# Attention and two feed-forward layers on one core: where the value sum's cast stands, and which engine converts the first weights

## The chip, the cores and the metric

The kernel runs on one core of a Trainium2 chip. The metric is the device time of one execution in microseconds (us), as the median of several runs. TensorE (PE) does the matrix products into PSUM, ScalarE (ACT) and VectorE (DVE) do the elementwise work, SyncE (SP) issues nearly all transfers. GpSimd (POOL) is idle but for the first microsecond.

## What is computed

```python
scores = scale * np.matmul(q, k.transpose(0, 1, 3, 2)) - np.log(S)
attn = 1.0 / (1.0 + np.exp(-scores))
attn_out = np.matmul(attn, v)              # batch 4, 12 heads, S = 448, head size 64
x = attn_out.transpose(0, 2, 1, 3).reshape(B * S, H * D)      # 1792 x 768
h = x @ w_in;   x = (h - np.tanh(h)) @ w_out                  # 768 -> 2048 -> 768
h = x @ w_in2;  out = (s * np.maximum(h, 0) ** 2 + b) @ w_out2
```

The weights arrive as 64-bit floats; all else is 32-bit.

## The kernel before

The work is done in two halves `sb` of two batches each. A half runs attention for 12 steps `i` (a step is one batch and a pair of heads), then `layer1`, then `layer2`, all on 896 rows. Every operation is recorded in the order in which the code is written, engine by engine (class `InOrder`, line 80, so all instructions of a profile carry the line L80). Products that have to be accurate are split: an operand is a rounded part `hi` and a rest `lo = t - hi`, and three products are summed.

One step `i` of attention (lines 490 to 506) runs, in this order:

- `qk(i, 0)` and `qk(i, 1)`: six products each into a PSUM tile `sc` and one sigmoid each on ScalarE, which writes `af`.
- in a few steps of the first half, `w_load`, `w_conv` or `w_split` for the first weights (line 495).
- `prep(i + 1)`: seven transposes of the next q and k into a PSUM tile `tqk`, two casts on ScalarE (`qt`, `kt`), and on VectorE two subtractions and the copy `qkf`. The tile is free again after that copy.
- `av(i - 1)` up to its `yield`: the value sum `o` of the step before, and a part `o2` of it in another bank.
- `qk(i, 3)`: four small products and a sigmoid of half the size.
- the rest of `av(i - 1)`: ScalarE copies `o2` to `half`, VectorE adds it to `o`, ScalarE casts `o` into `x`, VectorE subtracts for the rest of `x`.
- `qkv_load(i + 3)`: nine small transfers on SyncE's queue for the step after next but one.
- `qk(i, 2)`.

The tiles `sc` and `tqk` share three PSUM buffers of two banks (tag `two`), taken in turn; `o` and `o2` share two single banks (tag `one`). So each use of a `two` buffer waits for the reader of the use three before it: `prep(i + 2)` for the sigmoid of `qk(i, 2)`, `qk(i + 1, 0)` for the copy `qkf` of `prep(i + 1)`.

A weight piece of 128 x 768 goes through `w_load` (raw 64-bit words, 768 KB), `w_conv` (the 64-bit float to 32 bits: `wy` is the high word scaled, `wa` and `wf` put the bits together, and `wf` is stored to memory for the second half) and `w_split` (`whi`, `wlo`). The first pieces are converted while the first half's attention runs:

```python
for at, step, n in ((2, w_load, 1), (4, w_load, 2), (5, w_conv, 0), (6, w_split, 0), (7, w_load, 3), (7, w_conv, 1), (8, w_split, 1), (9, w_load, 4), (9, w_conv, 2)):
    if i == at:
        now(upto(step, n))
```

Of the kernel before, what the change touches and what calls it, by code (L numbers as in the profile page):

```python
# [9 lines left out]
F32 = mybir.dt.float32  # L10
F32R = mybir.dt.float32r
U32 = mybir.dt.uint32
AF = mybir.ActivationFunctionType
ALU = mybir.AluOpType
# [5 lines left out]
def tile_kernel(ctx, tc, q, k, v, w_in1, w_out1, w_in2, w_out2, s_in, b_in, out):  # L20
# [61 lines left out]
    pe, act, dve, pool, sp = (InOrder(e) for e in (nc.tensor, nc.scalar, nc.vector, nc.gpsimd, nc.sync))  # L82

    def banks(name):
        return ps_p.tile([P, 2, 512], F32, tag="two", name=name, bufs=3)
# [11 lines left out]
    def w_src(key):  # L97
        kind, layer, a, b = key
        if kind == "in":
            return words[2 * layer][:, a * P:(a + 1) * P, :].rearrange("(c p) f t -> p c f t", p=P)  # L100
        return words[2 * layer + 1][a * 2 * P:(a + 1) * 2 * P, b * HM:(b + 1) * HM, :].rearrange("(c p) f t -> p c f t", p=P)
# [6 lines left out]
    chunks = a_pass * (B // 2)  # L108
    scratch, raw_t, f_t, w_t = {}, {}, {}, {}

    def w_load(n):
        if n >= len(chunks):
            return
        key = chunks[n]
        if key not in scratch:
            t = w_p.tile([P, WE, 2], U32, tag="raw", name="raw", bufs=3)
            a = CC if key[0] == "in" else 2
            sp.dma_start(out=t.rearrange("p (a f) t -> p a f t", a=a), in_=w_src(key))
            raw_t[n] = t
        else:  # L120
            t = w_p.tile([P, WE], F32, tag="wf", name="wf", bufs=5)
            sp.dma_start(out=t, in_=scratch[key])
            f_t[n] = t

    def w_conv(n):

        if n >= len(chunks) or n in f_t:
            return
        key = chunks[n]
        r = raw_t.pop(n)
        a = w_p.tile([P, WE], U32, tag="wa", name="wa", bufs=2)
        y = w_p.tile([P, WE], F32, tag="wy", name="wy", bufs=2)
        t = w_p.tile([P, WE], F32, tag="wf", name="wf", bufs=5)
        act.activation(y, r[:, :, 1].bitcast(F32), AF.Copy, scale=2.0 ** -112)  # L140
        yield
        dve.tensor_scalar(a, r[:, :, 0], 29, None, op0=ALU.logical_shift_right)
        yield
        dve.scalar_tensor_tensor(out=a, in0=y.bitcast(U32), scalar=3, in1=a, op0=ALU.logical_shift_left, op1=ALU.bitwise_or)
        dve.scalar_tensor_tensor(out=t.bitcast(U32), in0=y.bitcast(U32), scalar=0x80000000, in1=a, op0=ALU.bitwise_and, op1=ALU.bitwise_or)
        scratch[key] = dram.tile([P, WE], F32, name=f"w{key[0]}{key[1]}_{key[2]}_{key[3]}")
        sp.dma_start(out=scratch[key], in_=t)
        f_t[n] = t

    def w_split(n):  # L150
        if n >= len(chunks):
            return
        t = f_t.pop(n)
        hi = w_p.tile([P, WE], F32R, tag="whi", name="whi", bufs=4)
        lo = w_p.tile([P, WE], F32R, tag="wlo", name="wlo", bufs=4)
        act.copy(hi, t)
        yield
        dve.tensor_tensor(out=lo, in0=t, in1=hi.bitcast(F32), op=ALU.subtract)
        w_t[n] = (hi, lo)

    done = {w_load: 0, w_conv: 0, w_split: 0}

    def upto(step, n):

        while done[step] <= n:
            yield from step(done[step]) or ()
            done[step] += 1

    def w_ahead(n, parts="ab"):

        yield from upto(w_load, n + 5)
        for part in parts:
            if part == "a":
                yield from upto(w_conv, n + 3)
            else:
                yield from upto(w_split, n + 2)

    def now(g):
        for _ in g:
            pass  # L180
# [7 lines left out]
    def split(hi, lo, t):  # L188
        act.copy(hi, t)
        dve.tensor_tensor(out=lo, in0=t, in1=hi.bitcast(F32), op=ALU.subtract)  # L190
# [67 lines left out]
    def qk(i, c):  # L258

        b = i // NP  # L260
        qt, kt = ready[i]
        sc = banks("sc")
        if c == NJ:

            f = flt.pop(i)
            kl, qf = (f[:, 0:RM], f[:, RM:]) if b % 2 else (f[:, S:], f[:, 0:S])
            for h in range(2):
                for e in range(2):
                    hs = slice(e * D, e * D + D)
                    pe.matmul(sc[h * RM:h * RM + RM, e, :SH], kl[hs], qf[hs, h * SH:h * SH + SH], start=True, stop=True)  # L270
            avs[i].append(g_p.tile([P, 2, 2, S], F32, tag="g", name="af", bufs=4))
            act.activation(avs[i][-1][:, 1, :, :SH], sc[:, :, :SH], AF.Sigmoid, bias=nlogs, scale=SCALE)
            return
        k0 = c * P if b % 2 else c * P + RM
        for n, (wi, xi) in enumerate(((0, 0), (0, 1), (1, 0))):
            for e in range(2):
                hs = slice(e * D, e * D + D)
                pe.matmul(sc[:, e, :S], kt[hs, wi, k0:k0 + P], qt[hs, xi], start=n == 0, stop=n == 2)
        if c == 0:
            avs[i].append(g_p.tile([P, 2, 2, S], F32, tag="g", name="af", bufs=4))  # L280
        act.activation(avs[i][-1][:, c % 2], sc[:, :, :S], AF.Sigmoid, bias=nlogs, scale=SCALE)

    def av(i):

        b, hp = i // NP, i % NP
        rv, af = raws.pop(i)["v"], avs.pop(i)
        o = ps_p.tile([P, 512], F32, tag="one", name="o", bufs=2)[:, :S]

        o2 = ps_p.tile([P, 512], F32, tag="one", name="o2", bufs=2)[:, :SH]
        for c in range(NJ):  # L290
            for e in range(2):
                pe.matmul(o[e * D:e * D + D], rv[:, e, c, :], af[c // 2][:, c % 2, e], start=c == 0, stop=False)
        for h in range(2):
            for e in range(2):
                ks = slice(h * RM, h * RM + RM)
                pe.matmul((o2 if h else o[:, :SH])[e * D:e * D + D], rv[ks, e, NJ, :], af[1][ks, 1, e, :SH], start=h == 1, stop=True)
        yield
        half = tmp_p.tile([P, WN], F32, tag="t1", name="half", bufs=2)[:, :SH]
        act.copy(half, o2)
        dve.tensor_tensor(out=o[:, SH:], in0=o[:, SH:], in1=half, op=ALU.add)  # L300
        if b % 2 == 0:
            x_t[b // 2, hp] = x_p.tile([P, 2, T2], F32R, tag="x", name="x1", bufs=CC)
        ns = slice(b % 2 * S, b % 2 * S + S)
        xt = x_t[b // 2, hp]
        split(xt[:, 0, ns], xt[:, 1, ns], o)
# [182 lines left out]
    for sb in range(B // 2):  # L488
        i0, i1 = sb * 2 * NP, (sb + 1) * 2 * NP
        for i in range(i0, i1):  # L490
            if i == 0 or i > i0:
                qk(i, 0)
                qk(i, 1)

            for at, step, n in ((2, w_load, 1), (4, w_load, 2), (5, w_conv, 0), (6, w_split, 0), (7, w_load, 3), (7, w_conv, 1), (8, w_split, 1), (9, w_load, 4), (9, w_conv, 2)):
                if i == at:
                    now(upto(step, n))
            if i + 1 < i1:
                prep(i + 1)
            a = av(i - 1) if i > i0 else iter(())  # L500
            next(a, None)
            qk(i, 3)
            now(a)
            qkv_load(i + 3)
            qk(i, 2)
            ready.pop(i)
        order = [(0, range(CC - 2)), lambda: now(av(i1 - 1)), (1, range(CC - 1)), (0, range(CC - 2, CC)), (1, [CC - 1])]

        turn[0] = 3
        x2 = layer1(sb, order)  # L510
        last = sb + 1 == B // 2
        order = [(0, range(CC - 1)), (1, range(CC - 1)), (0, [CC - 1]), (1, [CC - 1])]
        layer2(sb, x2, order, {} if last else {2: lambda: prep(i1), 4: lambda: qk(i1, 0), 6: lambda: qk(i1, 1)})
# [30 lines left out]
```

## Time and profile before

| | |
|---|---|
| time, median of 3 runs | 1125.86 us (1124.82 to 1127.56) |
| profiled execution, time | 1124.64 us |
| its span on the core | 1122.8 us |
| granted TensorE clock, mean | 1.0 |
| TensorE busy | 1098.6 us (98%) |
| VectorE busy | 585.5 us (52%) |
| ScalarE busy | 493.7 us (44%) |

Busy times come from one execution, which the hardware profiler recorded; its span leaves 1.84 us of its time outside. A busy TensorE is not TensorE at its peak, since products are pipelined and their ends are modelled; idle time on it is the better guide. The first half's attention runs from the start to about 95 us, the second half's from about 570 to 649 us.

### The profile page before, as it was taken

What the parts mean: (1) busy time and instruction counts of PE and PEld (TensorE: products, weight loads), DVE (VectorE), ACT (ScalarE), POOL (GpSimd) and SP (SyncE); (2) the same over time, 40 slices, a digit from 0 to 9 for tenths busy, and PEclk for the clock granted to TensorE, in tenths of its full rate; (3) what the DMA queues carried; (4) which work ended last, traced back from release to release, by engine and by line L of the source; (5) the groups of instructions that cost most, each with busy time, mean ns of one, the idle gap of its engine ahead of it and who ended that gap; (6) DMA issues with size and microseconds to landing.
All of it is one profiled execution on the core that took longest, in us unless ns stands there. A gap on an engine that the chain in (4) does not pass through costs nothing.

```text
span 1122.8 us, 15139 instructions
## 1 busy us (share of the span) xinstructions
PE 1098.6 (98%) x6077; PEld 949.4 (85%) x6077; DVE 585.5 (52%) x878; ACT 493.7 (44%) x782; POOL 0.7 (0%) x6
## 2 busy tenths in 40 slices
PE   8899999999999999999998899999999999999998
PEld 4446889888889999898964578898888899999998
DVE  3453656767787668686633332343434541434343
ACT  5775444242446563635356643332313363515060
POOL 0000000000000000000000000000000000000000
PEclk9999999999999999999999999999999999999999
DMA  4765454546455645454444301121211121211102
GB/s 112 201 152 148 156 185 154 169 146 192 127 169 168 203 136 183 133 189 130 167 113 113 79 29 57 48 66 43 71 43 46 54 71 43 60 53 57 57 15 99
DMA packets 115430, 124.47 MB, mean 111 GB/s; under 512 B 56480, under 2 KB 90784, under 8 KB 115360
## 3 DMA queue, kind: packets, MB, share of 16 engines
q1 hardware_dynamic: 114416, 123.27, 36.6%
q8 instruction: 48, 0.79, 0.3%
q10 hardware_dynamic: 944, 0.23, 0.1%
q14 instruction: 22, 0.18, 0.0%
HBM read 92.80 MB, written 30.67 MB: 110 GB/s over the span
## 4 chain that ended last, share of the span: by engine, by line
PE 92%; DMA 3%; DVE 2%; ACT 2%; SPq 1%; issue 1%; ACTq 0%; DVEq 0%
PE h L80 42%; PE z L80 21%; PE y L80 20%; PE o L80 6%; PE sc L80 2%; PE tqk L80 2%; SPq L80 1%; ACT af L80 1%; DMA rawq<-in_q_dram 1%; DMA rawv<-in_v_dram 1%; DMA rawk<-in_k_dram 1%; DMA win<-wf 1%; DVE wa L80 0%; DVE o L80 0%; DVE qt L80 0%
## 5 line engine op out<-in xcount | busy, mean ns | idle before, releaser
L80 PE MATMUL h<-x,whi 128*128 128x512 f32 (+1 forms) x1536 | 434.4, 363 | 0.0
L80 PEld LDWEIGHTS h<-x,whi 128*128 128x128 f32 x1536 | 283.4, 188 | 33.9 <-issue 1.3
L80 PE MATMUL h<-x,wlo 128*128 128x512 f32 (+1 forms) x768 | 279.8, 364 | 0.0
L80 PE MATMUL z<-whi,g 128*128 128x384 f32 x896 | 229.5, 334 | 0.0
L80 PE MATMUL y<-g,whi 128*128 128x512 f32 (+1 forms) x768 | 218.6, 366 | 0.2 <-DVE y L80 0.2
L80 ACT ACTIVATE t<-h 128x512 f32<-128x512 f32 (+1 forms) x128 | 69.6, 544 | 234.3 <-PE h L80 233.7
L80 PEld LDWEIGHTS z<-whi,g 128*128 128x128 f32 x896 | 162.0, 188 | 0.6 <-issue 0.6
L80 PEld LDWEIGHTS y<-g,whi 128*128 128x128 f32 x768 | 142.4, 188 | 17.7 <-DVE y L80 0.6
L80 PEld LDWEIGHTS h<-x,wlo 128*128 128x128 f32 x768 | 144.1, 188 | 15.2
L80 DVE TENSOR_TENSOR wlo<-wf,whi 128x768 fp32r<-128x768 f32 x128 | 122.0, 953 | 59.7 <-ACT whi L80 59.7
L80 ACT CAST whi<-wf 128x768 fp32r<-128x768 f32 x128 | 106.1, 833 | 101.9 <-DVE wf L80 58.0
L80 PE MATMUL z<-wlo,g 128*128 128x384 f32 x448 | 149.7, 334 | 0.0
L80 PE MATMUL y<-g,wlo 128*128 128x512 f32 (+1 forms) x384 | 140.9, 367 | 0.0
L80 DVE TENSOR_TENSOR g<-t,g 128x512 fp32r<-128x512 f32 (+1 forms) x128 | 79.9, 624 | 83.5 <-ACT g L80 83.5
L80 ACT ACTIVATE af<-sc,nlogs 128x896 f32<-128x896 f32 (+1 forms) x96 | 83.1, 919 | 48.4 <-PE sc L80 39.0
L80 ACT CAST g<-t 128x512 fp32r<-128x512 f32 (+1 forms) x128 | 72.7, 568 | 33.2 <-DVE t L80 30.9
L80 DVE TENSOR_TENSOR t<-h,t 128x512 f32<-128x512 f32 x64 | 39.9, 623 | 85.4 <-ACT t L80 85.4
L80 PEld LDWEIGHTS z<-wlo,g 128*128 128x128 f32 x448 | 84.1, 188 | 0.0
L80 PEld LDWEIGHTS y<-g,wlo 128*128 128x128 f32 x384 | 72.1, 188 | 8.9 <-DVE wlo L80 0.4
L80 DVE TENSOR_TENSOR z<-z 128x384 f32<-128x384 f32 x84 | 45.2, 554 | 65.8 <-PE z L80 65.8
L80 PE MATMUL o<-af,rawv 128*64 128x448 f32 (+1 forms) x480 | 72.4, 478 | 0.0
L80 DVE TENSOR_TENSOR y<-y 128x512 f32<-128x512 f32 x72 | 41.5, 618 | 58.0 <-PE y L80 58.0
(42 smaller groups left out, 674.9 us busy)
## 6 DMA issues: line engine op xcount, KB each, us to landing
raw<-in_moe_w_in_dram SPq DMA_DIRECT2D x32, 768.0 KB, 5.2
raw<-in_moe_w_out_dram SPq DMA_DIRECT2D x32, 768.0 KB, 4.8
win<-wf SPq DMA_DIRECT2D x32, 384.0 KB, 2.6
wout<-wf SPq DMA_DIRECT2D x32, 384.0 KB, 2.6
wf<-win SPq DMA_DIRECT2D x32, 384.0 KB, 3.0
wf<-wout SPq DMA_DIRECT2D x32, 384.0 KB, 3.0
rawq<-in_q_dram SPq DMA_DIRECT2D x48, 96.0 KB, 2.7
rawv<-in_v_dram SPq DMA_DIRECT2D x24, 192.0 KB, 2.7
```

The costliest lines, as they stand in the source:

```text
L80: return lambda *a, **kw: tc.keep_in_program_order(getattr(self.engine, name)(*a, **kw))
```

## The change

Two edits. In `av` a second `yield` stands behind the addition of `half`; the loop over the steps runs `av(i - 1)` in three pieces now, and the last piece (cast and subtraction) follows `qk(i, 2)` instead of going ahead of it. And the weight steps that run inside the attention loop get `alone=True`, with which the scaling to `wy` and the cast to `whi` are done on VectorE instead of ScalarE. Calls of the same steps from the layers are as before.

```diff
-    def w_conv(n):
+    def w_conv(n, alone=False):
...
-        act.activation(y, r[:, :, 1].bitcast(F32), AF.Copy, scale=2.0 ** -112)
+        if alone:
+            dve.tensor_scalar(y, r[:, :, 1].bitcast(F32), 2.0 ** -112, None, op0=ALU.mult)
+        else:
+            act.activation(y, r[:, :, 1].bitcast(F32), AF.Copy, scale=2.0 ** -112)
         yield
...
-    def w_split(n):
+    def w_split(n, alone=False):
...
-        act.copy(hi, t)
+        (dve.tensor_copy if alone else act.copy)(hi, t)
         yield
...
-    def upto(step, n):
+    def upto(step, n, **kw):
 
         while done[step] <= n:
-            yield from step(done[step]) or ()
+            yield from step(done[step], **kw) or ()
             done[step] += 1
...
         act.copy(half, o2)
         dve.tensor_tensor(out=o[:, SH:], in0=o[:, SH:], in1=half, op=ALU.add)
+        yield
         if b % 2 == 0:
...
-                    now(upto(step, n))
+                    now(upto(step, n, alone=True))
             if i + 1 < i1:
                 prep(i + 1)
             a = av(i - 1) if i > i0 else iter(())
             next(a, None)
             qk(i, 3)
-            now(a)
+            next(a, None)
             qkv_load(i + 3)
             qk(i, 2)
+            now(a)
             ready.pop(i)
```

How ScalarE's order moves, at the end of step `i` = 7 and in step 8 of the first half, in which the second split falls. The 128x2x224 sigmoid is that of `qk(i, 3)`, the 128x896 ones are `qk(i, 2)` and the next step's `qk(i + 1, 0)` and `qk(i + 1, 1)`; `x` is the value sum. Before:

```order
L80 ACTIVATE af<-sc,nlogs 128x2x224
L80 COPY half<-o_753 128x224
L80 CAST x_270<-o 128x448
L80 ACTIVATE af<-sc,nlogs 128x896 x3
L80 CAST whi<-wf 128x768
L80 CAST qt<-tqk 128x448
L80 CAST kt<-tqk 128x448
```

And now:

```order
L80 ACTIVATE af<-sc,nlogs 128x2x224
L80 COPY half<-o_753 128x224
L80 ACTIVATE af<-sc,nlogs 128x896
L80 CAST x_291<-o 128x448
L80 ACTIVATE af<-sc,nlogs 128x896 x2
L80 CAST qt<-tqk 128x448
L80 CAST kt<-tqk 128x448
```

The cast of `x` now stands behind the first of the three sigmoids, and the cast of `whi` is gone from this queue. TensorE's order of products and SyncE's order of transfers are the same as before.

VectorE's order around the first conversion and split, before:

```order
L80 TENSOR_TENSOR x_513<-o,x_513 128x448
L80 TENSOR_SCALAR wa<-raw 128x768
L80 SCALAR_TENSOR_TENSOR wa<-wy,wa 128x768
L80 SCALAR_TENSOR_TENSOR wf<-wy,wa 128x768
L80 TENSOR_TENSOR qt<-tqk,qt 128x448
L80 TENSOR_TENSOR kt<-tqk,kt 128x448
L80 COPY qkf<-tqk 128x512
L80 TENSOR_TENSOR o<-o,half 128x224
L80 TENSOR_TENSOR x_601<-o,x_601 128x448
L80 TENSOR_TENSOR wlo<-wf,whi 128x768
```

And now:

```order
L80 TENSOR_TENSOR x_534<-o,x_534 128x448
L80 TENSOR_SCALAR wy<-raw 128x768
L80 TENSOR_SCALAR wa<-raw 128x768
L80 SCALAR_TENSOR_TENSOR wa<-wy,wa 128x768
L80 SCALAR_TENSOR_TENSOR wf<-wy,wa 128x768
L80 TENSOR_TENSOR qt<-tqk,qt 128x448
L80 TENSOR_TENSOR kt<-tqk,kt 128x448
L80 COPY qkf<-tqk 128x512
L80 TENSOR_TENSOR o<-o,half 128x224
L80 TENSOR_TENSOR x_622<-o,x_622 128x448
L80 CAST whi<-wf 128x768
L80 TENSOR_TENSOR wlo<-wf,whi 128x768
```

The two operations that ScalarE did stand here now, each ahead of the one that reads its result; nothing else changes places.

On TensorE, the products of one value sum and what they wait for, the same before and now:

```order
L80 MATMUL o<-af,rawv 64x448 x6
L80 MATMUL o<-af,rawv 64x224 x2
L80 MATMUL o_332<-af,rawv 64x224 [waits DVE_49]
L80 MATMUL o_332<-af,rawv 64x224
L80 MATMUL sc<-qkf 64x224 [waits Activation_49]
```

Only the products into the second bank (`o_332`, the tile `o2`) wait for VectorE, whose subtraction was the last to read that bank.

## Rows read from the trace of the kernel before

**Rows 1.** Busy time by stretch: length, PE, PEld, DVE, ACT, POOL, clock, DMA.

```profile
20.00:95.00 75.00, 65.48 (x529) 35.44 (x527) 34.36 (x58) 52.89 (x84) 0.00 (x0) 1.00 0.68 172
105.00:560.00 455.00, 454.80 (x2337) 417.73 (x2336) 322.34 (x463) 210.80 (x325) 0.00 (x0) 1.00 0.51 161
575.00:649.00 74.00, 65.67 (x555) 37.11 (x553) 27.77 (x50) 49.65 (x81) 0.00 (x0) 1.00 0.39 95
```

**Rows 2.** Groups of TensorE in 580 to 645 us: busy, mean | idle before.

```profile
L80 PE MATMUL tqk<-ident,rawk 128*128 128x128 f32 x27 | 4.7, 285 | 5.6 <-DMA rawv<-in_v_dram 3.7 <-ACT af L80 1.9
L80 PE MATMUL tqk<-ident,rawq 128*128 128x128 f32 x27 | 4.6, 279 | 2.7 <-ACT af L80 2.7
```

**Rows 3.** One step in order of time: start, length, instruction [idle before].

```profile
588.24 0.55 PE L80 MATMUL tqk<-ident,rawq 128*128 128x128 f32 x3 [0.94 <-ACT af L80]
...
589.85 0.55 ACT L80 CAST qt<-tqk 128x448 fp32r<-128x448 f32 x1
...
591.94 0.68 DVE L80 COPY qkf<-tqk 128x512 f32<-128x512 f32 x1
...
592.47 2.12 PE L80 MATMUL sc<-qt,kt 64*128 64x448 f32 x18
592.67 0.63 ACT L80 ACTIVATE af<-sc,nlogs 128x448 f32<-128x448 f32 x1 [1.84 <-PE sc L80]
...
593.20 0.34 ACT L80 COPY half<-o 128x224 f32<-128x224 f32 x1
...
594.00 0.53 ACT L80 CAST x<-o 128x448 fp32r<-128x448 f32 x1 [0.46 <-DVE o L80]
594.43 1.91 ACT L80 ACTIVATE af<-sc,nlogs 128x896 f32<-128x896 f32 x2
594.57 0.62 DVE L80 TENSOR_TENSOR x<-o,x 128x448 fp32r<-128x448 f32 x1 [0.60 <-ACT x L80]
...
595.50 0.55 PE L80 MATMUL tqk<-ident,rawq 128*128 128x128 f32 x3 [0.91 <-ACT af L80]
```

**Rows 4.** TensorE in order of time, first stretch.

```profile
39.66 0.52 PE L80 MATMUL tqk<-ident,rawk 128*128 128x128 f32 x3 [0.40 <-DMA rawk<-in_k_dram]
...
77.17 0.55 PE L80 MATMUL tqk<-ident,rawk 128*128 128x128 f32 x3 [0.52 <-DMA rawq<-in_q_dram]
...
81.40 2.89 PE L80 MATMUL sc<-qt,kt 64*128 64x448 f32 x18
...
85.19 0.55 PE L80 MATMUL tqk<-ident,rawk 128*128 128x128 f32 x3 [0.91 <-ACT af L80]
...
86.11 3.02 PE L80 MATMUL o<-af,rawv 128*64 128x448 f32 x20
...
89.43 2.09 PE L80 MATMUL sc<-qt,kt 64*128 64x448 f32 x18
91.45 3.02 PE L80 MATMUL o<-af,rawv 128*64 128x448 f32 x20
```

**Rows 5.** Chain that ended last, 34 to 50 us: start, length, what.

```profile
35.23 4.29 DMA rawk<-in_k_dram
```

**Rows 6.** Groups of VectorE, whole span: busy us, mean ns of one | idle before.

```profile
L80 DVE TENSOR_TENSOR wlo<-wf,whi 128x768 fp32r<-128x768 f32 x128 | 122.0, 953 | 59.7 <-ACT whi L80 59.7
...
L80 DVE TENSOR_SCALAR wa<-raw 128x768 uint32<-128x768 uint32 x64 | 35.3, 552 | 0.0
```

**Rows 7.** VectorE in order of time, a converting step.

```profile
79.74 0.96 DVE L80 SCALAR_TENSOR_TENSOR wa<-wy,wa 128x768 uint32<-128x768 uint32 x1 [2.42 <-ACT wy L80]
...
82.68 0.68 DVE L80 COPY qkf<-tqk 128x512 f32<-128x512 f32 x1
```

**Rows 8.** SyncE's queue in order of time: start and time of the issues.

```profile
66.16 0.54 SPq L80 DMA_DIRECT2D raw<-in_moe_w_in_dram  x1
...
70.31 1.27 SPq L80 DMA_DIRECT2D rawk<-in_k_dram  x2
```

**Rows 9.** DMA issues of 70.9 to 71 us: count, KB each, median us to landing.

```profile
rawk<-in_k_dram SPq DMA_DIRECT2D x2, 96.0 KB, 4.4
```

More of the change, by code (lines that the diff above doesn't have):

```diff
@@ L109, in tile_kernel, with w_load @@
     scratch, raw_t, f_t, w_t = {}, {}, {}, {}
-    def w_load(n):
+    def w_load(n, alone=False):
         if n >= len(chunks):
```

## Prediction

> **What bounds the kernel now.** I first cut the span into stretches [rows 1]. Over the first layer and the first half's second layer (105 to 560 us) TensorE is busy 454.80 of 455 us: nothing that VectorE or ScalarE do there can be worth much. In the two attention stretches it is busy 65.48 of 75.00 us and 65.67 of 74.00 us. So 9.5 us and 8.3 us stand idle, 17.9 us together, and a change to attention can win little more than that. The granted clock is 1.00 (the 2.4 GHz level) in all three, so the clock is no term.
>
> Next, which instruction stands behind the idle time. In 580 to 645 us it is the transposes `tqk` alone, 5.6 + 2.7 = 8.3 us [rows 2]; every other group of TensorE there waits for nothing worth a term. The view names two causes, ScalarE's `af` and a load of v; but a transpose doesn't read v, so I take the nine waits (0.92 us in the mean) as one cause. One step in order of time shows it [rows 3]: `tqk` starts at 595.50 after 0.91 us idle, and the sigmoid of the score block `qk(i, 2)` (call it s2) starts at 594.43, 1.07 us before. The transposes need the PSUM buffer that s2 reads (three buffers of two banks, five uses a step). And s2 starts late because ScalarE, in order, does before it: the small sigmoid (592.67), the copy `half` (593.20), then waits 0.46 us for VectorE's addition of `half`, then casts `x` (594.00).
>
> The first attention stretch is mixed. There too `tqk` waits 0.91 us for ScalarE (85.19) [rows 4], but some transposes wait for their q and k [rows 5]: the load issued at 35.23 landed 4.29 us later, at 39.52, and the transposes followed at 39.66.
>
> **The change, part by part.**
>
> *The cast behind s2.* It moves 22 casts and 22 subtractions (one value sum each; two more stand elsewhere and are unmoved in effect), no DMA: SyncE's queue holds the same issues in the same order. After it s2 waits only for `half` and for its own products. `half` starts at 593.20, and a step between ScalarE instructions that wait for nothing is their length less about 0.1 us (592.67 to 593.20 for 0.63 us), so `half` releases ScalarE at 593.45. The products start at 592.47; six of the 18 take a third of 2.12 us plus pipeline, and end about 593.3. So s2 starts at about 593.45 instead of 594.43: 0.98 us earlier. The transposes would then start at 594.52. TensorE could itself reach them 2.02 us after 592.47, at 594.49, as the one step without transposes behind it shows (89.43 to 91.45) [rows 4]. The whole wait goes, 0.98 of at most 1.01 us.
>
> What is late next: the cast now lies between s2 and the next two sigmoids. ScalarE's order behind s2 becomes cast (0.90 later), two sigmoids (0.43 later, 0.90 each), cast of q (starts 594.35 + 0.43 + 1.80 = 596.58), cast of k. Before, the cast of q started 1.61 us behind `tqk` (589.85 against 588.24), now 2.06 us. VectorE's copy `qkf`, which frees the transposes' buffer for the next block c = 0, ended 591.94 + 0.68 = 592.62, 4.38 us behind `tqk`; now 4.83. Block c = 0 follows the six products of s2: a third of the 2.02 us behind 592.47, at 593.15, 4.91 us behind `tqk`. The margin of 0.53 us shrinks to 0.08 us, and some 0.15 us pass between a VectorE end and a TensorE start (as 0.14 us passed at 39.52 to 39.66). So I take 0.08 us a step as a new wait; bounds 0 and 0.3. A step gains 0.90 us.
>
> Another wait that could take its place: the subtraction that reads the value sum's bank moves to 594.35 + 0.57 = 594.92 and ends 595.54. The next value sum starts 0.92 us behind `tqk` (86.11 against 85.19) [rows 4], at 595.44. But the order of buffers shows that only its last four products (of 20 in 3.01 us) wait for VectorE; they come near 595.44 + 2.4 = 597.8. That hides it by 2.3 us.
>
> In the second half nine steps have the wait (27 transposes of q, three a step) [rows 2]: 9 x 0.90 = **8.1 us**.
>
> *VectorE alone converts.* Three conversions (a scaling to `wy`) and two splits (a cast to `whi`) move from ScalarE to VectorE, all in the first attention stretch. No row has either on VectorE. The lower bound is its single-source operation on the same raw data, 552 ns; the upper its two-source operation of the same width, 953 ns [rows 6]. I take 552 for both, to which they are nearest (one source, SBUF to SBUF): 3 x 0.55 + 2 x 0.55 = 2.8 us more on VectorE; at the upper bound 4.8 us. In exchange VectorE no longer waits 2.42 us for `wy` in a converting step [rows 7]. There `qkf` began at 82.68 and the score products took 2.89 us instead of 2.09 [rows 4], a stall of 0.8 us. Now the four operations (0.45 + 0.45 + 0.97 + 0.87 = 2.7 us after overlaps) start when the `x` subtraction ends, 2.09 us behind s2's start, and end near 4.8; with q, k and `qkf` (1.75 us) that is 6.6 us, and block c = 0 wants it at 1.07 + 4.91 = 5.98. Without cover a converting step still loses 0.6 to 0.8 us. The cover is the loads, next.
>
> *The first stretch.* The load behind the transposes at 39.66 is a fixed point: SyncE issues it on its own pace, so whatever is gained before is lost there. From there five steps to the transposes at 77.17, at 6.26 (85.19 to 91.45, unstalled) + 0.08 each and twice 0.8 for conversions, would lead to 39.66 + 31.7 + 1.6 = 73.0. But their k is issued from 70.31 on, in two pieces, the second near 70.95, behind a 768 KB piece of raw weights (66.16) [rows 8], and lands 4.4 us later [rows 9]: 75.35, so the transposes start near 75.5. VectorE has the third conversion done by then. The next transposes come at 75.5 + 6.34 = 81.8 instead of 85.19, and what follows is TensorE's own time: **3.3 us**.
>
> On this term a rule can be weighed. The row is 4.4 us for 96 KB beside weights. The Trainium skill, DMA: Bandwidth & Descriptors, section Anatomy of one DMA, fits one DMA (on GpSimd's path) as about 2.0 us plus its bytes over 436 GB/s; as an estimate 2.2 us for 96 KB, the transposes at 73.3 and a term of 5.5 us instead of 3.3. No run here shows a fit for this queue, and the row with weights in flight is twice that, so the row stands.
>
> *Sum.* 8.1 + 3.3 = 11.4 us off the profiled execution's 1124.64 us: 1113.2 us; off the median of 1125.86 us, 1114.5 us. I forecast between, **1113.8 us** (-1.1%). About 0.3% (3.4 us) is what a measurement of this kernel can tell from no change.
>
> **Rivals.**
> 1. *The loads take back all of the first stretch*: a later load, not only the one I pinned, arrives 3.3 us after it is wanted. For it: two stretches of the queue already end in waits for q or k. Against: the load behind the transposes at 85.19 wasn't waited for. Then 8.1 us remain: 1116.5 to 1117.8 us. Chance 0.12.
> 2. *The q and k chain becomes the bound*: `qkf` is late by 0.3 us instead of 0.08, say because ScalarE's operations don't overlap as I counted. Nine steps, and some two of the first stretch, lose 0.22 more: 2.4 us, about 1116. At 0.5 us late, 4.6 us, 1118. Chance 0.12.
> 3. *Slower*: the same chain, late by much more. It decides where `qkf` is later than 1.34 us in each of the 11 steps that gain: 11.4 + 3.4 = 14.8 us = 11 x 1.34. That would need the cast to push the chain by 1.8 us, where its place in the queue is 0.43 us long. The time would be 1128 and more. Chance 0.03.
> 4. *s2 doesn't start earlier*, since its products, not ScalarE's queue, arrive last. For it: both come within 0.2 us of 593.4 by my count, so an error there is soon visible. Against: a full 0.98 us would have to vanish. Then 0 to 3 us, 1122 to 1125. Chance 0.05.
> 5. *The first stretch isn't held by loads*: landings are shorter without the present collisions, and all of its steps gain. To the 3.3 us come up to 2.5 (73.0, TensorE's own pace, instead of 75.5), or 4 if the fixed point at 39.66 falls too: 1109 to 1111. For it: only loads beside raw weights are seen late. Against: the weights stay where they are in the queue. The fit of the Trainium skill quoted above speaks for it. Chance 0.08.
> My forecast, 10 to 13 us gained: 0.60.
>
> So faster by over 0.3%: 0.60 + 0.12 + 0.12 + 0.08 = 0.92; within: 0.05; slower: 0.03. The range 1109.5 to 1119 takes in rivals 1, 2 and most of 5 and leaves out 3 and 4; the likeliest case alone is 1111.5 to 1115.5.
>
> **What would show it.** Right: in the second attention stretch TensorE idles under 1.5 us before `tqk` instead of 8.3, a step takes 6.3 to 6.4 us instead of 7.26 (588.24 to 595.50), and ScalarE's row has s2 directly behind `half`, its wait now on the cast with no one behind it that matters. Waits of `sc` for `qkf` appear, near 0.1 us. In the first stretch transposes wait for loads of q and k, 2 us and more before the one near 75.5. `wy` and `whi` on VectorE take 0.5 to 0.6 us. Wrong: the step stays above 6.7 us; a wait of the value sum's products for VectorE; the last transposes of the first stretch at 85; or idle time after 105 us, which would mean that weights come late.

## The result, and the profile after

The changed kernel takes 1114.19 us (median of 4 runs, 1113.2 to 1114.63) against 1125.34 us (4 runs, 1124.77 to 1127.56) of the kernel before: a ratio of 0.9896, with a 95% interval of 0.9879 to 0.9913. The forecast was 1113.8 us, faster. The profiled execution took 1113.2 us, which is what the sum gave for it, and its span is 1111.4 us against 1122.8.

The stretches of the kernel after, with the columns of [rows 1]; the third ends 4 us earlier than there and begins 10 us earlier:

```profile
20.00:95.00 75.00, 69.68 (x562) 39.39 (x559) 38.20 (x66) 50.37 (x82) 0.00 (x0) 0.98 0.69 172
105.00:560.00 455.00, 454.80 (x2340) 417.45 (x2339) 322.42 (x463) 208.40 (x322) 0.00 (x0) 1.00 0.51 162
565.00:645.00 80.00, 79.62 (x643) 46.03 (x642) 31.51 (x57) 57.37 (x94) 0.00 (x0) 1.00 0.39 96
```

The middle is as it was. In the second attention stretch 0.38 us of idle time are left, and in the first 5.3 of 9.5. The groups of TensorE in 575 to 632 us, which answer to [rows 2], have no idle time ahead of the transposes at all, where 8.3 us stood:

```profile
L80 PE MATMUL tqk<-ident,rawk 128*128 128x128 f32 x27 | 4.8, 285 | 0.0
L80 PE MATMUL tqk<-ident,rawq 128*128 128x128 f32 x27 | 4.6, 279 | 0.0
```

One step in order of time, which answers to [rows 3]:

```profile
582.21 1.02 ACT L80 ACTIVATE af<-sc,nlogs 128x896 f32<-128x896 f32 x1
...
583.11 0.54 ACT L80 CAST x<-o 128x448 fp32r<-128x448 f32 x1
...
583.36 0.55 PE L80 MATMUL tqk<-ident,rawq 128*128 128x128 f32 x3
583.52 1.94 ACT L80 ACTIVATE af<-sc,nlogs 128x896 f32<-128x896 f32 x2
...
584.27 3.02 PE L80 MATMUL o<-af,rawv 128*64 128x448 f32 x20
...
585.31 0.57 ACT L80 CAST qt<-tqk 128x448 fp32r<-128x448 f32 x1
...
587.42 0.68 DVE L80 COPY qkf<-tqk 128x512 f32<-128x512 f32 x1
587.59 2.14 PE L80 MATMUL sc<-qt,kt 64*128 64x448 f32 x18
...
588.55 1.02 ACT L80 ACTIVATE af<-sc,nlogs 128x896 f32<-128x896 f32 x1
...
589.66 0.55 PE L80 MATMUL tqk<-ident,rawq 128*128 128x128 f32 x3
```

The step takes 589.66 - 583.36 = 6.30 us; it was 7.26. The sigmoid s2 starts 1.15 us ahead of the transposes that need its buffer (582.21 against 583.36), so that they follow the products before them at once. The cast of `x` stands behind s2, and no one waits for it: the value sum at 584.27 takes its 3.02 us unstalled. The score products take 2.14 us, 0.05 more than unstalled [rows 4]; this is what remains of the wait for `qkf`.

TensorE in the first stretch, which answers to [rows 4]:

```profile
39.05 0.52 PE L80 MATMUL tqk<-ident,rawq 128*128 128x128 f32 x3 [2.44 <-DMA rawq<-in_q_dram]
39.81 0.55 PE L80 MATMUL tqk<-ident,rawk 128*128 128x128 f32 x3 [0.25 <-DMA rawk<-in_k_dram]
...
40.51 4.52 PE L80 MATMUL o<-af,rawv 128*64 128x448 f32 x20
...
47.37 0.55 PE L80 MATMUL tqk<-ident,rawk 128*128 128x128 f32 x3
...
53.14 1.49 PE L80 MATMUL sc<-qt,kt 64*128 64x448 f32 x12 [0.66 <-DVE qkf L80]
54.56 0.55 PE L80 MATMUL tqk<-ident,rawk 128*128 128x128 f32 x3
...
75.67 0.52 PE L80 MATMUL tqk<-ident,rawk 128*128 128x128 f32 x3 [1.31 <-ACT af L80]
...
81.91 0.55 PE L80 MATMUL tqk<-ident,rawk 128*128 128x128 f32 x3
...
88.28 3.02 PE L80 MATMUL o<-af,rawv 128*64 128x448 f32 x20
```

Its last value sum starts at 88.28 instead of 91.45, 3.17 us earlier. The wait at 75.67 is put down to a sigmoid that ends then; but the reader of the buffer, the sigmoid s2 at 73.20, had ended at 74.22. The transfers of k show the other candidate (an issue in SyncE's queue: start and time; then issues at 70.5 to 71.2 us: count, KB each, median us to landing), answering to [rows 8, 9]:

```profile
70.22 1.27 SPq L80 DMA_DIRECT2D rawk<-in_k_dram  x2
```

```profile
rawk<-in_k_dram SPq DMA_DIRECT2D x2, 96.0 KB, 4.9
```

The second piece is issued at about 70.87 and lands 4.8 to 4.9 us later, at 75.7. So I read this wait as one for k, and experiment e5 tests that.

VectorE's groups in 20 to 95 us, which answer to [rows 6]; these are the two that are new on it:

```profile
L80 DVE TENSOR_SCALAR wy<-raw 128x768 f32<-128x768 f32 x3 | 1.7, 555 | 0.0
L80 DVE CAST whi<-wf 128x768 fp32r<-128x768 f32 x2 | 1.1, 550 | 0.0
```

### The profile page after: what moved, and what is told of

The parts are those of the page before. It is cut to its first block, busy times and chain, and to the rows that moved or that the text cites. A ratio compares the mean times of both kernels' runs of the same rounds, so it can differ in the third digit from the quotient of the medians.

```text
span 1111.4 us, 15136 instructions
## 1 busy us (share of the span) xinstructions
PE 1097.1 (99%) x6077; PEld 948.7 (85%) x6077; DVE 588.2 (53%) x883; ACT 487.6 (44%) x777; POOL 0.7 (0%) x6
## 4 chain that ended last, share of the span: by engine, by line
PE 95%; DVE 2%; SPq 2%; DMA 1%; ACT 1%; issue 0%; DVEq 0%; ACTq 0%
PE h L80 42%; PE z L80 21%; PE y L80 20%; PE o L80 6%; PE sc L80 4%; PE tqk L80 2%; SPq L80 2%; DMA rawk<-in_k_dram 1%; DVE wa L80 0%; ACT af L80 0%; DVE x L80 0%; ACT x L80 0%; DVE wf L80 0%; DVE y L80 0%; DVE wlo L80 0%
## 5 line engine op out<-in xcount | busy, mean ns | idle before, releaser
L80 ACT ACTIVATE af<-sc,nlogs 128x896 f32<-128x896 f32 (+1 forms) x96 | 86.0, 929 | 51.0 <-PE sc L80 41.6
L80 PE MATMUL o<-af,rawv 128*64 128x448 f32 (+1 forms) x480 | 75.0, 491 | 0.0
```

What stands on the lines that cost most here:

```text
L80: return lambda *a, **kw: tc.keep_in_program_order(getattr(self.engine, name)(*a, **kw))
```

## The experiments

The theory under test: the second stretch gains because s2 no longer queues behind the cast; the first gains until the loads of q and k hold it, and there the second edit is worth next to nothing, because the loads cover what it saves. The rival: the second edit has a good part of the gain, or the chain of ScalarE and VectorE up to `qkf`, not the loads, holds the first stretch. Ratios are to the kernel before, in runs beside each experiment (1124.89 to 1125.07 us in the median, one of 1125.92 beside e3); a change is against the changed kernel unless said otherwise.

**e1: the first edit alone.** ScalarE keeps the scaling to `wy` and the cast to `whi`.

```diff
-                    now(upto(step, n, alone=True))
+                    now(upto(step, n))
```

> The cast behind the sigmoid of qk(i, 2), with the weights of the attention loop converted as before (scaling and cast on ScalarE). Theory A, two edits with separate shares: the second attention stretch keeps its whole gain (8.4 us, steps of 6.32 us). In the first stretch the scaling still stands before the cast of q on ScalarE, and with the value sum's cast now ahead of both, a converting step takes about 8.1 us (before 8.03, in the changed kernel 7.19) and a splitting step about 7.0 (6.3), so the transposes of 75.67 come near 77.7 and the first stretch gains nothing: minus 0.7 to plus 1 us. In all 7.7 to 9.4 us under the kernel before, ratio 0.992 to 0.993. Theory B, the conversions are covered by the loads wherever they are done: the same 11.2 us as the changed kernel, ratio 0.990.

Measured: 1113.79 us, ratio 0.9899 (0.9886 to 0.9913), the same as with both edits. TensorE's waits in 40 to 90 us (engine, for what: us in total, times, longest):

```profile
PE tqk L80 <- DMA rawk<-in_k_dram: 0.9, 2, 0.7
PE sc L80 <- ACT half L80: 0.5, 2, 0.2
```

A converting step took 7.46 us (transposes 47.34 to 54.80) and k was waited for again (0.65 us of the 0.9, at 76.05), half as long as with both edits: the pin took in what the steps lost. The last value sum starts at 88.82, 0.54 us behind that of the changed kernel. Theory A, by which the second edit had a visible part of the gain, is refuted.

**e2: the second edit alone.** The cast stands ahead of s2 again.

```diff
-            next(a, None)
+            now(a)
             qkv_load(i + 3)
             qk(i, 2)
-            now(a)
```

> VectorE alone converts, the cast stays ahead of the sigmoid as before. Theory A: nothing changes in the second stretch (8.3 us idle); in the first the three converting steps fall from 8.03 to 7.26 us, 2.3 us in all, ratio 0.998. Theory B: 0, ratio 1.000. If the two shares simply add to the changed kernel's 11.2 us, this and the cast alone sum to it; by theory A they sum to 10 to 11.7.

Measured: 1123.64 us, ratio 0.9989 (0.998 to 0.9998). TensorE in the first stretch:

```profile
68.67 0.55 PE L80 MATMUL tqk<-ident,rawk 128*128 128x128 f32 x3 [0.94 <-ACT af L80]
...
76.63 0.52 PE L80 MATMUL tqk<-ident,rawk 128*128 128x128 f32 x3 [1.64 <-DMA rawk<-in_k_dram]
...
83.87 0.55 PE L80 MATMUL tqk<-ident,rawk 128*128 128x128 f32 x3 [0.92 <-ACT af L80]
```

Converting or not, a step takes 7.27 us (transposes 54.13, 61.40, 68.67), the wait for s2 included, where a converting one took 8.03 before, and at 76.63 k takes part of it back. The last value sum starts at 90.15, 1.30 us earlier than before. So the second edit is worth 1.3 us by itself, where the pin leaves less than I expected, and nothing measurable on top of the first.

**e3: the raw weights' transfers one in every second step**; the conversions stay where they were. In the changed kernel only the first two go out as a pair (at 30.66 us), the next ones at 46.13, 66.35 and 80.98; here they go out at 31.18, 44.51, 58.79, 72.68 and 87.19.

```diff
-... in ((2, w_load, 1), (4, w_load, 2), (5, w_conv, 0), (6, w_split, 0), (7, w_load, 3), (7, w_conv, 1), (8, w_split, 1), (9, w_load, 4), (9, w_conv, 2)):
+... in ((2, w_load, 0), (4, w_load, 1), (5, w_conv, 0), (6, w_split, 0), (6, w_load, 2), (7, w_conv, 1), (8, w_split, 1), (8, w_load, 3), (9, w_conv, 2), (10, w_load, 4)):
```

> The changed kernel with the transfers of the raw weights issued one in every second step instead of in pairs. Theory S (SyncE's pace of issues pins the first stretch, and not the bytes of the raw weights beside the loads): the 2.44 us wait for rawq before the transposes at 39.05 shrinks to under 1 us and the product with v after it keeps its 3.0 us, but the pins at 75.67 and 81.91 stay within 0.7 us and the time within 1 us of the changed kernel's 1114. Theory W (the raw weights' bytes hold the loads up): the waits at 66 to 82 go too and the time falls to 1109 to 1112.

Measured, one execution: 1110.87 us, against 1113.2 of the changed kernel's profiled one. The largest of TensorE's waits in 22 to 90 us:

```profile
PE tqk L80 <- DMA rawk<-in_k_dram: 4.4, 6, 1.7
PE tqk L80 <- ACT x L80: 0.7, 2, 0.4
PE sc L80 <- DVE qkf L80: 0.6, 1, 0.6
```

Neither theory holds whole. The time is theory W's, but by it the waits at 66 to 82 us were to go, and k is still waited for at 79.86 (1.02 us), and six times in all, 4.4 us. The wait of 2.44 us at 39 is gone (0.31 us), as both said, and the last value sum starts at 86.09, 2.2 us earlier: where the 768 KB transfers stand was part of the pin. Taking the pair apart and issuing the later pieces earlier are not separated here.

**e4: the cast later still**, behind the next step's casts of q and k. This asks whether the bank of `o2` is a real constraint, which I had put 2.3 us away.

```diff
+        late = iter(())
         for i in range(i0, i1):
...
+            now(late)
             a = av(i - 1) if i > i0 else iter(())
...
             qk(i, 2)
-            now(a)
+            late, a = a, None
             ready.pop(i)
+        now(late)
```

> The cast and subtraction of the value sum go further back, behind the casts of the next q and k. This frees ScalarE for q and k by 0.43 us a step, but the subtraction that empties the bank of o2 lands behind the copy of q and k on VectorE, 1.7 us after the next o2 products could start. Theory, that the bank of o2 is hidden by only 2.3 us: TensorE waits for VectorE at o, a step takes about 8.0 us instead of 6.32, and the time is 1130 to 1145 us, slower than both kernels. Rival, that this bank never matters and only the q and k chain does: steps of 6.26 us and 1113 us or less.

Measured, one execution: 1134.33 us, slower than before. TensorE in 575 to 640 us, by groups, and two of its steps:

```profile
L80 PE MATMUL o<-af,rawv 64*64 64x224 f32 x64 | 9.0, 375 | 7.3 <-DVE x L80 7.3
```

```profile
591.39 0.55 PE L80 MATMUL tqk<-ident,rawq 128*128 128x128 f32 x3
...
596.36 0.41 PE L80 MATMUL o<-af,rawv 64*64 64x224 f32 x2 [1.05 <-DVE x L80]
...
599.29 0.55 PE L80 MATMUL tqk<-ident,rawq 128*128 128x128 f32 x3
```

The last four products of the value sum now wait 1.05 us for the subtraction of `x`, and a step takes 7.90 us, near the 8.0 of the theory. So the bank is held until that subtraction, as the order of waits said, and four places further back in ScalarE's queue (two sigmoids and two casts) turn the gain into a loss.

**e5: the transfers of v on GpSimd's queue.** SyncE then issues six transfers a step instead of nine.

```diff
-            dma = act if i == 0 and nm == "k" else sp
+            dma = act if i == 0 and nm == "k" else pool if nm == "v" else sp
```

> The changed kernel, with the three transfers of v of each step issued on GpSimd's queue instead of SyncE's (9 issues a step on SyncE become 6). Theory P, the pace at which SyncE issues sets when q and k of the first stretch arrive: SyncE runs ahead, the waits near 36 to 40 us and before 75.67 shrink, and the first stretch gains 3 to 6 us more: 1108 to 1111 us. Theory W, the collision with the raw weights on the DMA engines sets it: the landings stay 4 us and more, 0 to 2 us more, 1112 to 1114. Slower if GpSimd's issues come later than v is needed: waits of o for v.

Measured: 1108.85 us, ratio 0.9855 (0.9842 to 0.9869), 5.3 us less. TensorE's waits in 22 to 84 us, all of them:

```profile
PE sc L80 <- DVE qkf L80: 1.9, 3, 0.7
```

No transposes wait for a load any more, as theory P had it. The step that in the changed kernel ended at 75.67 with a wait of 1.31 us has none here (63.55 to 69.81, 6.26 us), with the same work on ScalarE: so the wait was k's, and not the sigmoid's that the view names. The k of these transposes is issued at 62.80, 7.0 us ahead of them, where it was issued 5.45 us ahead (70.22 to 75.67):

```profile
62.80 1.26 SPq L80 DMA_DIRECT2D rawk<-in_k_dram  x2
```

What is left are the three converting steps, 0.6 us each. At the start something was lost: the first transposes begin at 7.75 instead of 5.31, behind the identity matrix that GpSimd now makes after its issues.

**e6: one more copy on ScalarE behind the cast** (128x448), to measure how near the `qkf` chain is.

```diff
         split(xt[:, 0, ns], xt[:, 1, ns], o)
+        act.copy(zero, zero)
```

> The changed kernel with one more ScalarE copy (128x448, about 0.43 us after overlap, its result unused) right behind the value sum's cast, so the casts of the next q and k come 0.43 us later in every step. Theory, the chain over those casts to VectorE's copy qkf has no margin left (0.08 us short in the prediction): each step of the second stretch grows from 6.32 to 6.7 us or more, 10 steps 4 us, the first stretch 0 to 2 us, in all 1117 to 1120 us. Rival, TensorE alone sets the step and the chain still has margin: steps of 6.3 to 6.4 us, 1114 to 1115 us.

Measured, one execution: 1115.71 us, 2.5 us more than the profiled one of the changed kernel (1113.2) and less than the first expectation. TensorE and VectorE in two steps:

```profile
590.48 0.55 PE L80 MATMUL tqk<-ident,rawq 128*128 128x128 f32 x3
...
594.99 0.68 DVE L80 COPY qkf<-tqk 128x512 f32<-128x512 f32 x1
...
595.82 1.50 PE L80 MATMUL sc<-qt,kt 64*128 64x448 f32 x12 [0.23 <-ACT half L80]
...
597.25 0.55 PE L80 MATMUL tqk<-ident,rawk 128*128 128x128 f32 x3
...
601.29 0.68 DVE L80 COPY qkf<-tqk 128x512 f32<-128x512 f32 x1
601.48 2.12 PE L80 MATMUL sc<-qt,kt 64*128 64x448 f32 x18
...
603.53 0.55 PE L80 MATMUL tqk<-ident,rawk 128*128 128x128 f32 x3
```

Steps of 6.77 and 6.28 us alternate. In the long one the score products wait at 595.82, 0.15 us after `qkf` ends (595.67). The view names `half`, but the order of products and of what each waits for is that of the changed kernel, where these products wait for `qkf`. So the chain has no margin left: the copy pushes the casts of q and k back by 0.47 us (its start at 590.64 to the next sigmoid's at 591.11), and a step pays it whole. But only every second step does. The sigmoid s2 doesn't wait for the products that are late, so ScalarE is ahead by as much in the next step, where `qkf` begins 4.04 us behind the transposes instead of 4.51. Both expectations missed this: the first had every step pay, the second none.

**e7: e5 without the second edit** (its diff is that of e1). With the loads out of the way the second edit should have a price.

> v on GpSimd's queue as in the run before, and the weights of the attention loop converted on ScalarE and VectorE as in the kernel before: what the second edit is worth once the loads no longer cover the first stretch. Theory, the loads covered it: now the converting and splitting steps show, with 7.0 to 7.5 us and 6.75 us against 7.18 and 6.35 us with VectorE alone, 1 to 2 us more than the 1108.85 us of that run: 1110 to 1111 us. Rival, the edit is worth nothing anywhere: 1108.9 us.

Measured: 1110.12 us, ratio 0.9869 (0.9853 to 0.9886), 1.3 us more than e5. The five steps that e5 does in 34.00 us (transposes 42.98 to 76.98) take 34.96 here (43.48 to 78.44). They also begin 0.50 us later, but that arose at the start, where the two kernels do the same (first value sum at 19.14 against 18.65). The 0.96 us lie in the two splitting steps, 6.75 us each against 6.27 and 6.26; the three converting steps are equal in sum (7.43, 7.01 and 7.02 us against 7.11, 7.19 and 7.17). So behind the first edit the cast to `whi` on VectorE is worth 0.5 us a split and the scaling to `wy` nothing, and in the changed kernel the loads hide the 1 us.

**e8: e5 with the identity matrix made ahead of GpSimd's issues.**

```diff
+    make_identity(nc, ident)
     for i, what in ((0, "qk"), (1, "qk"), (0, "v"), (1, "v"), (2, "qkv")):
...
     act.activation(warm, nlogs, AF.Sigmoid)
-    make_identity(nc, ident)
```

> v on GpSimd's queue, with the identity matrix made ahead of GpSimd's first transfers. In the run before the first transposes waited until 7.75 us for the identity (5.31 in the changed kernel). Theory, this wait is on the path: it goes, and the time falls by up to 2.4 us to 1106.5 to 1108 us; less where the loads of the third pair of heads are the next to be waited for, near 16 us. Rival: no change, 1108.9 us.

Measured: 1106.98 us, ratio 0.9841 (0.9826 to 0.9856), 1.9 us less than e5; the first transposes begin at 5.38. The converting steps wait for `qkf` as in e5, 1.9 us in all.

**e9: e8, with the last operation of a conversion behind `qkf`.** In a converting step `wf` is computed after `prep(i + 1)`.

```diff
+        if alone:
+            yield
         dve.scalar_tensor_tensor(out=t.bitcast(U32), ...)
...
+            rest = iter(())
...
-                    now(upto(step, n, alone=True))
+                    g = upto(step, n, alone=True)
+                    if step is w_conv:
+                        for _ in range(3):
+                            next(g)
+                        rest = g
+                    else:
+                        now(g)
...
                 prep(i + 1)
+            now(rest)
```

> As the run with the identity first, and of the three conversions the last of four VectorE operations goes behind the copy qkf. Theory: the 0.59 to 0.66 us that the score products wait for qkf in a converting step go, 1.9 us in all, since VectorE has 2.0 us idle ahead of the subtraction of q. 1.5 to 2 us below that run: 1105 to 1106 us. Rival: the operation now holds up the addition of half and with it the value sum's cast; then 0 or some tenths slower.

Measured: 1104.44 us, ratio 0.9817 (0.9802 to 0.9832), the fastest version. Its busy times in 20 to 85 us, with the columns of [rows 1]:

```profile
20.00:85.00 65.00, 65.00 (x547) 37.60 (x540) 37.31 (x64) 49.94 (x82) 21.06 (x33) 1.00 0.71 191
```

TensorE has no idle time left there, and every step takes 6.31 to 6.34 us, converting or not. It saved 2.5 us in the medians and 2.3 us between the profiled executions, more than the 1.9 us that the view counts as waits: a converting step of e5 takes 7.16 us in the mean (7.11, 7.19, 7.17), 0.84 over 6.32, and three of them make 2.5.

## Why the prediction was right, step by step

**s2 and the second stretch (8.1 us predicted).** Right. Between the transposes at 569.19 before (566.18 now) and the last value sum of the stretch, at 645.34 before (633.92 now), the kernel gained 11.42 - 3.01 = 8.41 us. Nine steps, between the transposes at 570.76 and at 627.60, take 6.32 us in the mean, where the prediction had 6.34 (6.26 unstalled and 0.08 of new wait); the new wait is about 0.06 us. Rival 4 (s2 not earlier) is refuted by the row of s2 itself. Rival 2 asked for `qkf` 0.3 us late, and the score products' 2.14 us rule that out; e6 shows that its mechanism is real, that the margin is used up as worked out (the 0.15 us from a VectorE end to a TensorE start, which the prediction took from a landing load, is 0.15 there, 595.67 to 595.82), and that its price is half of what the prediction set, since every second step goes free.

**VectorE's prices (0.55 us each, 2.8 in all).** Right: 555 and 550 ns. A converting step of the changed kernel takes 7.19 us (47.37 to 54.56), 0.93 more than an unstalled one, where 0.6 to 0.8 and the 0.08 of every step were predicted: a little low. The view calls only 0.66 of it a wait.

**The first stretch (3.3 us predicted, 3.17 measured).** The mechanism is right: the pin stood at 75.67, predicted 75.5, and the next transposes came at 81.91, predicted 81.8; e5 shows that a transfer makes the pin. Rival 1 fell with that, and rival 5 (no pin) too, as far as the present queue goes; e5 shows what it would have been worth. One step on the way was wrong without harm: the prediction said that the clock is no term, but TensorE reached the pin with 1.31 us to wait and not 2.5 (75.5 against 73.0), since a value sum took 4.52 us at a lower clock (last section). It did no harm because a pin with more waiting than that stood behind it; ahead of TensorE's own steps at the end it would have cost its 1.5 us.

**Why the loads come late.** The prediction named the bytes of the raw weights beside them. The runs show two parts, which overlap. Issuing the weights one by one and in part earlier (e3, one execution) moved the last value sum by 2.2 us; taking three of nine issues from SyncE (e5) moved it by 5.0 us (83.24 against 88.28), with the weights behind the same steps as before. SyncE's nine issues take about 6 us of a step of 6.3, and more when weights are issued among them (two rows of its queue, the loads of q of two steps, with a raw weight and a store between them):

```profile
60.40 1.27 SPq L80 DMA_DIRECT2D rawq<-in_q_dram  x2
...
66.35 0.59 SPq L80 DMA_DIRECT2D raw<-in_moe_w_in_dram  x1
67.04 0.49 SPq L80 DMA_DIRECT2D win<-wf  x1
67.57 1.51 SPq L80 DMA_DIRECT2D rawq<-in_q_dram  x2
```

That is 7.17 us from step to step, with TensorE wanting 6.3: the queue of issues falls behind. It waited for other engines and transfers for only 3.2 us in all in 20 to 95 us. In e5 v's bytes leave SyncE's queue too, but what is left in it does not land sooner: k takes 3.1 us in the median of 20 to 90 us, 2.9 in the changed kernel. What e5 changed is when k is issued.

The Trainium skill, DMA: Bandwidth & Descriptors, section Issuing engines are not separate DMA queues, says that issuing from several engines only saves the time to initiate a transfer, usually small beside the transfer itself. The trace agrees: the landings did not get shorter, and 0.6 us an issue is small beside 2.9 us to landing. But nine issues in one queue fill a step, and three fewer were enough to end every wait for a load. The same page's fit for one DMA (section Anatomy of one DMA, on GpSimd's path), as an estimate 2.2 us for 96 KB, was weighed in the prediction and left aside for the row of 4.4 us; the landing after the change was 4.9 us, and the time came out by the row.

**The second edit.** The prediction let two converting steps cost 1.6 us over unstalled ones and hid that behind the loads; it gave the edit no gain of its own. e1 agrees (no difference), and e7 puts its worth at about 1 us where no load covers it, all in the splits, to which the prediction gave no gain.

**What was left out, and luck.** The sum 8.41 + 3.17 is 11.58 us; the span gained 11.4. Between the two attention stretches 0.16 us went back: 477.90 us from 88.28 to 566.18, against 477.74 from 91.45 to 569.19. That the forecast sum of 11.4 us is met to 0.1 us is luck: the second stretch gave 0.3 us more than its term, the first 0.1 us less, and the middle took back 0.2.

## What to carry to other kernels

When an engine in order releases a buffer late, look at what stands ahead of the releasing instruction and who needs that: here a cast that no one waited for stood ahead of a sigmoid that everyone waited for, and exchanging them gave 0.9 us in every step; but count the next reader too, since the same cast four places further back cost 0.6 us a step against the kernel before. Before adding up gains over a stretch, look for instructions in it whose time is set by another queue: up to such a pin gains and losses alike vanish, and only what follows it counts. Count the issues of a queue as work of its own; the cheapest further gain was to give a third of them to an idle engine.

## What was not expected of the hardware

TensorE's clock fell for a few microseconds inside the first stretch. In the changed kernel the value sum behind the wait of 2.44 us took 4.52 us instead of 3.02, and another, at 17.31 behind a wait of 1.31 us, took 4.18. The stretches of 9 us around them, with the columns of [rows 1]:

```profile
14.00:23.00 9.00, 7.64 (x53) 3.81 (x51) 1.92 (x4) 3.50 (x7) 0.00 (x0) 0.81 0.43 97
38.00:47.00 9.00, 7.71 (x51) 3.97 (x53) 2.15 (x4) 3.03 (x6) 0.00 (x0) 0.81 0.58 134
```

A mean of 0.81 means part of the stretch at the lower level of 1.2 GHz. In e1 the clock fell too, behind a wait of 2.34 us (the value sum at 40.91 took 4.08 us). In the kernel before both stretches stand at 1.00, the second behind a wait of 1.23 us. The length of the wait doesn't decide alone: in e1 the engine waited 1.66 us at 16.54 and kept 1.00, in the changed kernel 1.31 us at 75.67 and kept its 3.02 us. What does decide stays open. In the changed kernel the loss (1.2 and 1.5 us on the two value sums) did not reach the end as far as the trace shows, since a wait for a load followed each time, of 2.44 us at 39.05 and of 1.31 us at 75.67.

Which of the three `two` buffers a tile takes is part of the timing, too: they are not always taken in turn. Where ScalarE does the scaling, the first score block of the next step takes a buffer in a converting step that doesn't wait for `qkf`, and the second block one that does. In the kernel before this shows in the weight loads of TensorE (PEld) for the score products that start at 81.40, beside `qkf` at 82.68 [rows 7]; the first four weights of the next step's first block are loaded before it begins, and only the six of the second block wait for it:

```profile
82.28 0.30 PEld L80 LDWEIGHTS sc<-qt,kt 64*128 64x128 f32 x4 [0.39 <-ACT af L80]
...
83.41 0.50 PEld L80 LDWEIGHTS sc<-qt,kt 64*128 64x128 f32 x6 [0.41 <-DVE qkf L80]
```

e1 and e7 show the same order. In the changed kernel and in e5 the first block waits (0.66 us at 53.14). That is not in the edit; it is probably why the converting steps of e1 came out shorter than I had worked out, and why those of e7 are no longer than those of e5. No run tests it by itself.
